# Planner changes in a threshold-attention and GELU kernel: weight loads in one chain, tied to later pairs, and other ranks

## The chip, the cores and the metric

The kernel runs on one core of a Trainium2 chip. The metric is the device time of one execution in microseconds (us). The kernel before takes 1434.29 us, the median of three runs (1433.63 to 1434.62). A profile of one execution gives a span of 1431.2 us.

A core has five engines that run side by side: TensorE (PE, matrix products), VectorE (DVE), ScalarE (ACT), GpSimd (POOL) and SyncE (SP). Here GpSimd issues the loads of the weights, and SyncE nearly all other transfers. Each engine runs its own list of instructions; semaphores make one wait for another.

## What is computed

```python
# attention: batch 8, heads 8, sequence 576, head_dim 64, float32
scores = q @ k.transpose(0, 1, 3, 2) / sqrt(64)
thresh = max(scores, axis=-1) - tau
scores = where(scores >= thresh, scores, -1e9)
scores = scores - max(scores, axis=-1)
attn = exp(scores);  attn = attn / (sum(attn, axis=-1) + 1e-9)
a = attn @ v
# bridge: heads side by side -> x of 4608 tokens x 512
h = x @ w_in                        # 512 x 2048
g = h * 1 / (1 + exp(-1.702 * h))
out = g @ w_out                     # 2048 x 512
```

Both weights arrive as 64-bit floats. The kernel itself turns them into 32-bit ones.

## The kernel before

Two heads make a pair, and there are 32 pairs, 4 to a batch element. For each pair the kernel transposes q and k (VectorE), makes the transposed scores (TensorE) in four tiles of 128 keys and a tail of 64 per head, copies them to SBUF (ScalarE), reduces the maxima (VectorE), sends the threshold row through DRAM to all partitions (SyncE; pairs 0 to 7), subtracts it (VectorE), masks with a steep Prelu and takes the exponential (ScalarE), multiplies with v and, for pairs 0 to 4, with ones for the denominators (TensorE), and places the scaled result in `xT` (VectorE). Whenever 512 tokens are complete, a block of the feed-forward part follows: 64 matmuls with w_in, 16 GELUs, 64 matmuls with w_out.

The Python program first lists all pieces of work as tasks and then runs a planner, a small event simulation with an assumed cost for each task. Whenever an engine of the simulation is free, the ready task with the lowest rank is emitted on it. The planner thus decides the order of instructions on each engine, once, while the program is built. The waits on the chip come from the data that instructions share, not from the planner's edges.

```python
    limits = {"psA": 3, "psM": 2, "s_m": 8, "s_t": 2, "io": 2, "xT": 3, "mb": 1,
              "raw0": 1, "raw1": 1, "qkT0": 1, "qkT1": 1, "v_m": 2, "w64": 2, "mbt": 1, "row": 1, "kd": 1}
    # ... cut ...
    EARLY = {
        "lower_rows": -1.16,
        "values": 0.42,
        "exps": 0.63,
        "load_qk": -0.91,
        "prep": -1.45,
        "load_v": 0.65,
        "over_groups": -1.04,
        "sub": -0.29,
    }
    LATER = {"in_groups": 0.38}

    def task(engine, cost, rank, f, *a, after=(), take=(), give=(), lag=0.06):
        if 0 <= rank < LAST:
            rank += (EARLY if a[0] < 2 * NPAIR else LATER).get(f.__name__, 0.0)
        tasks.append((engine, cost, rank, f, a, [x for x in after if x is not None],
                      take, give, lag))
        return len(tasks) - 1
```

A piece of weights (128 x 512 elements) is loaded twice, the second time shifted by three bytes, and converted in four steps: exponent bits (VectorE), power of two (ScalarE), fraction (two VectorE instructions), product (VectorE). Sixteen pieces belong to w_in and sixteen to w_out. The loads land in four staging areas, which lie in the still unused `w_out`, or in two buffers `w64`:

```python
    def load_w(i):
        # ... cut: t and t3 are a staging area or a w64 buffer ...
        nc.gpsimd.dma_start(out=t.rearrange("p c w -> p (c w)"), in_=dram.bitcast(U32))
        nc.gpsimd.dma_start(
            out=t3.rearrange("p c w -> p (c w)").bitcast(U8)[:, 0 : 8 * WC - 3],
            in_=dram.bitcast(U8)[:, 3 : 8 * WC],
        )
    # ... cut ...
    ready_w = []
    for i in range(len(pieces)):
        rank = 3.61 + 0.42 * i / n_in if i < n_in else 4.11 + 0.57 * (i / n_in - 1)
        # ... cut ...
        x = stage(i)
        place = ("w64",) if x is None else (f"stage{x}",)
        a = task("POOL", 2.4, rank, load_w, i, take=place, lag=5.0)
        e = task("DVE", 0.43, rank, cv_ex, i, after=[a])
        m = task("ACT", 0.79, rank, cv_power, i, after=[e])
        a = task("DVE", 1.14, rank, cv_frac, i, after=[e])
        over = [ready_w[y] for y in range(i) if i >= n_in and stage(y) == (i - n_in) // PER_STAGE]
        ready_w.append(task("DVE", 0.7, rank - 1.01, cv_end, i, after=[a, m] + over, give=place))
```

Loads and transposes of a pair, and its softmax:

```python
        lq = task("SP", 2.0, r - 2.0, load_qk, n, 0, q0, take=own(n, "raw0"), lag=2.0)
        lk = task("SP", 2.0 if n else 0.1, r - 2.0, load_qk, n, 1, q1, take=own(n, "raw1"), lag=2.0)
        lv = task("SP", 2.1, r - 1.2, load_v, n, take=("v_m",), lag=2.0)
        pq = task("DVE", 0.77, r, prep, n, 0, after=[lq], take=own(n, "qkT0"), give=own(n, "raw0"))
        pk = task("DVE", 0.77, r, prep, n, 1, after=[lk], take=own(n, "qkT1"), give=own(n, "raw1"))
        # ... cut: scores, copies, maxima, threshold row ...
            a = task("DVE", ..., r, sub, n, t, after=subs[-1:], ...)
            a = task("ACT", 0.68 if tail else 1.16, r, mask, n, t, after=[a])
            ws.append(task("ACT", 0.87 if tail else 1.34, r, exps, n, t, after=[a]))
```

The scratch of pairs 1 and 3 lies in the still unused `gT`, so the profile shows their tiles under that name. Matmuls are `L344` and `L337` (scores, `ps`), `L476` (values `pv` and denominators `den`), `L555` (w_in, `hps`) and `L574` (w_out, `ops`).

Of the kernel before, what the change touches and what calls it, by code (L numbers as in the profile page):

```python
# [30 lines left out]
def kernel(  # L31
# [32 lines left out]
    NPAIR = H // 2  # L64
    NKT = 4
# [18 lines left out]
    psA = ctx.enter_context(tc.tile_pool(name="psA", bufs=3, space=bass.MemoryType.PSUM))  # L84
# [6 lines left out]
    kd = const.tile([P, P], FP32, name="kd")  # L91
    v_t = [const.tile([P, 2, D], FP32, name=f"v_t{i}") for i in range(2)]
# [13 lines left out]

    tasks = []
    limits = {"psA": 3, "psM": 2, "s_m": 8, "s_t": 2, "io": 2, "xT": 3, "mb": 1,
              "raw0": 1, "raw1": 1, "qkT0": 1, "qkT1": 1, "v_m": 2, "w64": 2, "mbt": 1, "row": 1, "kd": 1}
    for x in ("raw0", "raw1", "qkT0", "qkT1", "mb"):  # L110
        limits[x + "_apart"] = 1
    limits["s_m_apart"] = NKT
# [1 line left out]


    EARLY = {
        "lower_rows": -1.16,
        "values": 0.42,
        "exps": 0.63,
        "load_qk": -0.91,  # L120
        "prep": -1.45,
        "load_v": 0.65,
        "over_groups": -1.04,
        "sub": -0.29,
    }
    LATER = {"in_groups": 0.38}

    def task(engine, cost, rank, f, *a, after=(), take=(), give=(), lag=0.06):
        if 0 <= rank < LAST:
            rank += (EARLY if a[0] < 2 * NPAIR else LATER).get(f.__name__, 0.0)  # L130
# [70 lines left out]
    def own(n, *pools):  # L201
        return tuple(x + "_apart" for x in pools) if n in APART else pools
# [33 lines left out]
    n_in = len(pieces)  # L236
# [294 lines left out]
    def cuts(b):  # L531

        return sorted({0, SH, S} | {x for x in range(-b * S % BLK, S, BLK)})
# [89 lines left out]
    BY_DMA = 8  # L623
    LEAD = 6

    ready_w = []
# [58 lines left out]
    for n in range(NP):  # L685
        gate = per_pair * (n - LEAD)
        after = ffn[gate : gate + 1] if gate >= 0 else []
        r = float(n)

        slow = 1.2 if n < NPAIR else 1.0  # L690
        q0, q1 = (nc.sync, nc.scalar) if n == 0 else (nc.sync, nc.sync)
        lq = task("SP", 2.0, r - 2.0, load_qk, n, 0, q0, take=own(n, "raw0"), lag=2.0)
        lk = task("SP", 2.0 if n else 0.1, r - 2.0, load_qk, n, 1, q1, take=own(n, "raw1"), lag=2.0)
        lv = task("SP", 2.1, r - 1.2, load_v, n, take=("v_m",), lag=2.0)
        pq = task("DVE", 0.77, r, prep, n, 0, after=[lq], take=own(n, "qkT0"), give=own(n, "raw0"))
        pk = task("DVE", 0.77, r, prep, n, 1, after=[lk], take=own(n, "qkT1"), give=own(n, "raw1"))
        pd = task("ACT", 0.5, r, prep_kd, n, after=[pk], take=("kd",))
        mx = []
        for t in range(NKT + 1):
            tail = t == NKT  # L700
            copies = []
            for c in range(1 if tail else 2):

                a = task(
                    "PE", (0.97 if tail else 0.53) * slow, r, scores, n, t, c,
                    after=[pq, pk] + ([pd] if tail else []) + after,
                    take=("psA", "s_t") if tail else ("psA",) + (own(n, "s_m") if c == 0 else ()),
                    give=own(n, "qkT0", "qkT1") + ("kd",) if tail else (),
                )
                after = [a]  # L710
                copies.append(task("ACT", 0.65, r, keep, n, t, c, after=[a], give=("psA",)))
            mx.append(task("DVE", 0.76 if tail else 1.37, r, in_groups, n, t, ALU.max, after=copies))
        a = task("DVE", 0.78, r, over_tiles, n, ALU.max, after=mx)
        a = task("DVE", 0.78, r, over_groups, n, ALU.max, after=[a])
        if n < BY_DMA:
            a = task("DVE", 0.5, r, lower_rows, n, after=[a, tau_done], take=("row",))
            a = task("SP", 0.35, r, row_out, n, after=[a], lag=2.3)
            m = task(
                "SP", 1.5, r, row_in, n, after=[a], take=own(n, "mb") + ("mbt",), give=("row",),
                lag=4.0,  # L720
            )
        else:
            a = task("DVE", 0.7, r, lower, n, after=[a, tau_done])
            m = task("DVE", 1.38, r, spread_max, n, after=[a], take=own(n, "mb"))
        ws, subs = [], [m]
        for t in range(NKT + 1):
            tail = t == NKT
            a = task(
                "DVE", (0.76 if n < BY_DMA else 1.5) if tail else 1.36, r, sub, n, t, after=subs[-1:],
                give=own(n, "mb") + (("mbt",) if n < BY_DMA else ()) if tail else (),  # L730
            )
            subs.append(a)
            a = task("ACT", 0.68 if tail else 1.16, r, mask, n, t, after=[a])
            ws.append(task("ACT", 0.87 if tail else 1.34, r, exps, n, t, after=[a]))
        back = own(n, "s_m") * NKT + ("s_t",)
        every = range(NKT + 1)
        if n < NPAIR:

            pv = den = None
            for t in every:  # L740
                first = t == 0
                den = task(
                    "PE", 1.1 * slow, r, sums_by_pe, n, [t], True, after=[ws[t], den],
                    take=("psM", "psM") if first else (),
                )
                pv = task(
                    "PE", 1.1 * slow, r, values, n, [t], after=[ws[t], den, pv, lv],
                    take=("psA",) if first else (), give=(back[t],) if t < NKT else ("s_t", "v_m"),
                )
            a = task("DVE", 1.22, r, one_row, n, after=[den], give=("psM", "psM"))  # L750
        else:
            pv = task("PE", 4.85, r, values, n, every, after=ws + [lv], take=("psA",), give=("v_m",))
# [53 lines left out]
```

## Time and profile before

| engine | busy us | share of the span |
|---|---|---|
| TensorE | 1380.6 | 96% |
| VectorE | 970.2 | 68% |
| ScalarE | 658.9 | 46% |
| GpSimd | 35.8 | 3% |

Each matmul with w_in or w_out shows as two records of 0.43 us each. The page cuts the span into 40 slices of 35.8 us. In them TensorE is busy 3, 7, 7 and 9 tenths, and from there on 9 (that is, 90% or more) in nearly every slice. So the first 120 us, in which the first pairs are worked on and the weights are loaded and converted, are the only stretch with much idle time on TensorE.

A line of the profile by groups names the source line, the engine, the operation, what it writes and reads, and how often. A line of waits names the waiting engine and instruction and, behind the arrow, what ended the wait.

### The profile page before, as it was taken

What the parts mean: (1) busy time and instruction counts of PE and PEld (TensorE: products, weight loads), DVE (VectorE), ACT (ScalarE), POOL (GpSimd) and SP (SyncE); (2) the same over time, 40 slices, a digit from 0 to 9 for tenths busy, and PEclk for the clock granted to TensorE, in tenths of its full rate; (3) what the DMA queues carried; (4) which work ended last, traced back from release to release, by engine and by line L of the source; (5) the groups of instructions that cost most, each with busy time, mean ns of one, the idle gap of its engine ahead of it and who ended that gap; (6) DMA issues with size and microseconds to landing.
All of it is one profiled execution on the core that took longest, in us unless ns stands there. A gap on an engine that the chain in (4) does not pass through costs nothing.

```text
span 1431.2 us, 13710 instructions
## 1 busy us (share of the span) xinstructions
PE 1380.6 (96%) x4936; PEld 650.2 (45%) x4936; DVE 970.2 (68%) x1629; ACT 658.9 (46%) x886; POOL 35.8 (3%) x78
## 2 busy tenths in 40 slices
PE   3779989999999999999999999999999999999998
PEld 2344434444444444444444444444444444444443
DVE  3999999888778888888887887788778710100200
ACT  3786655555455555555555554455445500100100
POOL 2012220000000000000000000000000000000000
PEclk8999999999999999999999999999999999999999
DMA  9468673211111111111111111111110000000000
GB/s 246 99 191 259 204 254 94 67 33 25 33 40 33 26 25 40 33 33 25 33 40 33 25 31 34 40 25 25 33 40 8 1 8 22 0 7 22 0 7 22
DMA packets 205707, 79.31 MB, mean 55 GB/s; under 512 B 192840, under 2 KB 192840, under 8 KB 205640
## 3 DMA queue, kind: packets, MB, share of 16 engines
q1 hardware_dynamic: 196072, 44.60, 14.4%
q0 software_dynamic: 7200, 33.55, 6.6%
q8 instruction: 39, 0.64, 0.2%
q10 hardware_dynamic: 2368, 0.30, 0.1%
q14 instruction: 28, 0.23, 0.1%
HBM read 68.93 MB, written 9.47 MB: 55 GB/s over the span
## 4 chain that ended last, share of the span: by engine, by line
PE 88%; DVE 6%; SPq 2%; DMA 2%; ACT 1%; issue 1%; DVEq 0%; ACTq 0%
PE ops L574 34%; PE hps L555 34%; PE pv L476 9%; PE ps L344 9%; PE ps L337 2%; SPq L214 2%; DVE s_m L447 1%; DVE part L377 1%; DMA mb<-row 1%; ACT gT L462 1%; ACT gT L458 1%; DMA row<-flat 0%; PE den L476 0%; DVE w_in L309 0%; DVE gT L447 0%
## 5 line engine op out<-in xcount | busy, mean ns | idle before, releaser
L574 PE MATMUL ops<-w_out,gT 128*128 128x512 f32 x1152 | 507.8, 596 | 5.0 <-DVE w_out L309 5.0
L555 PE MATMUL hps<-xT,w_in 128*128 128x512 f32 x1152 | 506.4, 595 | 0.3 <-DVE gT L566 0.3
L377 DVE TRANSPOSE_TENSOR_REDUCE part<-s_m 128x36 f32<-128x1152 f32 x228 | 303.5, 1358 | 101.8 <-ACT s_m L363 96.8
L574 PEld LDWEIGHTS ops<-w_out,gT 128*128 128x128 f32 x1152 | 216.2, 190 | 273.8 <-issue 263.5
L555 PEld LDWEIGHTS hps<-xT,w_in 128*128 128x128 f32 x1152 | 216.3, 190 | 267.9 <-issue 256.4
L566 DVE SCALAR_TENSOR_TENSOR gT<-th,hps 128x512 f32<-128x512 f32 x144 | 97.5, 677 | 234.8 <-ACT th L563 234.2
L363 ACT COPY s_m<-ps 128x576 f32<-128x576 f32 x240 | 138.8, 650 | 155.4 <-PE ps L344 153.9
L563 ACT ACTIVATE th<-hps 128x512 f32<-128x512 f32 x144 | 85.2, 592 | 217.4 <-PE hps L555 191.6
L458 ACT ACTIVATE s_m<-s_m 128x1152 f32<-128x1152 f32 x120 | 137.6, 1153 | 62.5 <-DVE s_m L447 62.1
L462 ACT ACTIVATE s_m<-s_m,shift,scl 128x1152 f32<-128x1152 f32 x120 | 160.5, 1343 | 2.4
L447 DVE TENSOR_TENSOR s_m<-s_m,mb 128x1152 f32<-128x1152 f32 x120 | 156.2, 1351 | 5.0 <-DMA mb<-row 4.3
L344 PE MATMUL ps<-qkT 64*128 64x288 f32 x960 | 144.6, 432 | 12.7 <-DVE qkT L320 12.2
L581 ACT ACTIVATE osb<-ops 128x512 f32<-128x512 f32 x36 | 21.4, 594 | 233.5 <-PE ops L574 233.3
L344 PEld LDWEIGHTS ps<-qkT 64*128 64x128 f32 x960 | 83.9, 189 | 91.4 <-issue 52.5
L476 PE MATMUL pv<-s_m,v_m 128*64 128x288 f32 x960 | 124.9, 413 | 0.0
L476 PEld LDWEIGHTS pv<-s_m,v_m 128*64 128x64 f32 x960 | 67.2, 138 | 64.0 <-issue 12.6
L377 DVE TRANSPOSE_TENSOR_REDUCE part_t<-s_t 128x18 f32<-128x576 f32 x59 | 44.2, 749 | 0.7 <-ACT s_t L363 0.2
L543 DVE TENSOR_TENSOR xT<-pv,rc 128x288 f32<-128x288 f32 (+8 forms) x96 | 28.3, 350 | 17.0 <-PE pv L476 15.7
L337 PE MATMUL ps<-qkT,kd 128*128 128x288 f32 x120 | 36.8, 429 | 0.3 <-ACT s_m L363 0.3
L476 PE MATMUL pv<-s_t,v_t 128*64 128x288 f32 x256 | 36.5, 406 | 0.0
L452 DVE TENSOR_TENSOR s_t<-s_t,mb 64x576 f32<-64x576 f32 x48 | 36.0, 749 | 0.3
L325 ACT COPY kd<-qkT 64x64 f32<-64x64 f32 x60 | 14.5, 241 | 45.6 <-DVE qkT L320 45.2
(81 smaller groups left out, 621.4 us busy)
## 6 DMA issues: line engine op xcount, KB each, us to landing
out_dram<-osb SPq DMA_DIRECT2D x36, 256.0 KB, 2.0
q_raw<-in_q_dram SPq DMA_DIRECT2D x120, 72.0 KB, 2.2
k_raw<-in_k_dram SPq DMA_DIRECT2D x116, 72.0 KB, 2.3
v_m<-in_v_dram SPq DMA_DIRECT2D x64, 128.0 KB, 2.4
w_out<-in_moe_w_in_dram POOLq DMA_DIRECT2D x12, 512.0 KB, 9.1
w<-in_moe_w_out_dram POOLq DMA_DIRECT2D x12, 512.0 KB, 4.8
w_out<-in_moe_w_in_dram POOLq DMA_DIRECT2D x12, 511.6 KB, 10.0
w64s<-in_moe_w_out_dram POOLq DMA_DIRECT2D x12, 511.6 KB, 5.8
```

The costliest lines, as they stand in the source:

```text
L337: nc.tensor.matmul(ps[:, i, 0:SH], lhsT=kd, rhs=qT[:, ts(i, SH)], start=True, stop=True,)
L344: nc.tensor.matmul(ps[:, h, 0:SH], lhsT=kT[ts(h, D), ts(t, P)], rhs=qT[ts(h, D), ts(c, SH)], start=True, stop=True,)
L363: nc.scalar.copy(out=o, in_=pss.pop((n, t, c))[:, :, 0:SH])
L377: nc.vector.tensor_reduce(out=o, in_=i, axis=AXL.X, op=op, apply_transpose=True)
L447: nc.vector.tensor_tensor(out=s, in0=s, in1=mb, op=ALU.subtract)
L458: nc.scalar.activation(out=s, in_=s, func=AF.Prelu, alpha=STEEP)
L462: nc.scalar.activation(out=s, in_=s, func=AF.Exp, scale=scl, bias=shift)
L476: nc.tensor.matmul(o[c][ts(h, D), 0:SH], lhsT=lhsT, rhs=rhs, start=(t == 0), stop=(t == NKT),)
L555: nc.tensor.matmul(hidden[j], lhsT=w_in[:, c, ts(j, P)], rhs=xTs[blk][:, c, :], start=(c == 0), stop=(c == NDC - 1),)
L563: nc.scalar.activation(out=ths[j], in_=hidden[j], func=AF.Tanh, scale=GELU_SCALE / 2)
L566: nc.vector.scalar_tensor_tensor(out=gT[j], in0=ths.pop(j), scalar=1.0, in1=hidden.pop(j), op0=ALU.add, op1=ALU.mult)
L574: nc.tensor.matmul(acc[i], lhsT=gT[j][:, ts(i, P)], rhs=w_out[:, j, :], start=(j == 0), stop=(j == NFC - 1),)
```

## The change

It touches the planner alone: ranks, assumed costs, and edges between tasks.

- Every weight load gets an edge from the load before it. In the planner the first three also wait for the transposed k of the third pair (n = 2), and the next three for that of the fourth (n = 3). This is meant to keep the weights out of the way of the first pairs.
- The ranks of all weight work are new, and the final product no longer runs ahead of its piece's rank.
- The table of rank offsets for the first eight pairs has new values and two new entries.
- The planner learns of buffers that it did not count: `rc` and the two `v_t`. The assumed cost of value and denominator matmuls of the first four pairs and the assumed latency of the threshold row are raised.

```diff
     limits = {"psA": 3, "psM": 2, "s_m": 8, "s_t": 2, "io": 2, "xT": 3, "mb": 1,
-              "raw0": 1, "raw1": 1, "qkT0": 1, "qkT1": 1, "v_m": 2, "w64": 2, "mbt": 1, "row": 1, "kd": 1}
+              "raw0": 1, "raw1": 1, "qkT0": 1, "qkT1": 1, "v_m": 2, "w64": 2, "mbt": 1, "row": 1, "kd": 1, "rc": 1, "v_t0": 1, "v_t1": 1}
     EARLY = {
-        "lower_rows": -1.16,
+        "lower_rows": -1.89,
         "values": 0.42,
         "exps": 0.63,
         "load_qk": -0.91,
         "prep": -1.45,
-        "load_v": 0.65,
-        "over_groups": -1.04,
+        "load_v": 1.46,
+        "mask": 0.88,
+        "over_groups": -1.9,
         "sub": -0.29,
+        "one_group": 0.95,
     }
 ... cut: an empty table CV is added ...
-        rank = 3.61 + 0.42 * i / n_in if i < n_in else 4.11 + 0.57 * (i / n_in - 1)
+        rank = 3.04 + 0.51 * i / n_in if i < n_in else 2.15 + 2.2 * (i / n_in - 1)
-        a = task("POOL", 2.4, rank, load_w, i, take=place, lag=5.0)
+        a = task("POOL", 2.4, rank, load_w, i, after=w_loads[-1:], take=place, lag=5.0)
+        w_loads.append(a)
-        ready_w.append(task("DVE", 0.7, rank - 1.01, cv_end, i, after=[a, m] + over, give=place))
+        ready_w.append(task("DVE", 0.7, rank, cv_end, i, after=[a, m] + over, give=place))
-        lv = task("SP", 2.1, r - 1.2, load_v, n, take=("v_m",), lag=2.0)
+        lv = task("SP", 2.1, r - 1.2, load_v, n, take=("v_m", v_tail), lag=2.0)
+        if n in (2, 3):
+            for a in w_loads[3 * (n - 2) : 3 * (n - 1)]:
+                tasks[a][5].append(pk)
-            a = task("SP", 0.35, r, row_out, n, after=[a], lag=2.3)
+            a = task("SP", 0.35, r, row_out, n, after=[a], lag=2.8)
             m = task(
                 "SP", 1.5, r, row_in, n, after=[a], take=own(n, "mb") + ("mbt",), give=("row",),
-                lag=4.0,
+                lag=5.0,
             )
-                    "PE", 1.1 * slow, r, sums_by_pe, n, [t], True, after=[ws[t], den],
+                    "PE", 1.32 * slow, r, sums_by_pe, n, [t], True, after=[ws[t], den],
-                    "PE", 1.1 * slow, r, values, n, [t], after=[ws[t], den, pv, lv],
+                    "PE", 1.32 * slow, r, values, n, [t], after=[ws[t], den, pv, lv],
-        a = task("DVE", 1.07, r, spread_sums, n, after=[a])
+        a = task("DVE", 1.07, r, spread_sums, n, after=[a], take=("rc",))
-            "DVE", 1.1, r, place_x, n, after=[a, pv], take=("xT",) * len(new), give=("psA",)
+            "DVE", 1.1, r, place_x, n, after=[a, pv], take=("xT",) * len(new), give=("psA", "rc")
 ... cut: the same buffers are given back with v_tail in two more places ...
```

More of the change, by code (lines that the diff above doesn't have):

```diff
@@ L121 @@
         "prep": -1.45,
-        "load_v": 0.65,
-        "over_groups": -1.04,
+        "load_v": 1.46,
+        "mask": 0.88,
+        "over_groups": -1.9,
         "sub": -0.29,
+        "one_group": 0.95,
     }
-    LATER = {"in_groups": 0.38}
+    LATER = {
+        "in_groups": 0.38,
+    }
+    CV = {
+    }
     def task(engine, cost, rank, f, *a, after=(), take=(), give=(), lag=0.06):
         if 0 <= rank < LAST:
-            rank += (EARLY if a[0] < 2 * NPAIR else LATER).get(f.__name__, 0.0)
+            rank += CV.get(f.__name__, 0.0) + (EARLY if a[0] < 2 * NPAIR else LATER).get(f.__name__, 0.0)
         tasks.append((engine, cost, rank, f, a, [x for x in after if x is not None],
@@ L624 @@
     LEAD = 6
-    ready_w = []
+    ready_w, w_loads = [], []
     for i in range(len(pieces)):
-        rank = 3.61 + 0.42 * i / n_in if i < n_in else 4.11 + 0.57 * (i / n_in - 1)
+        rank = 3.04 + 0.51 * i / n_in if i < n_in else 2.15 + 2.2 * (i / n_in - 1)
         if not wide:
@@ L693 @@
         lk = task("SP", 2.0 if n else 0.1, r - 2.0, load_qk, n, 1, q1, take=own(n, "raw1"), lag=2.0)
-        lv = task("SP", 2.1, r - 1.2, load_v, n, take=("v_m",), lag=2.0)
+        v_tail = f"v_t{n % 2}"
+        lv = task("SP", 2.1, r - 1.2, load_v, n, take=("v_m", v_tail), lag=2.0)
         pq = task("DVE", 0.77, r, prep, n, 0, after=[lq], take=own(n, "qkT0"), give=own(n, "raw0"))
         pk = task("DVE", 0.77, r, prep, n, 1, after=[lk], take=own(n, "qkT1"), give=own(n, "raw1"))
+        if n in (2, 3):
+            for a in w_loads[3 * (n - 2) : 3 * (n - 1)]:
+                tasks[a][5].append(pk)
         pd = task("ACT", 0.5, r, prep_kd, n, after=[pk], take=("kd",))
@@ L746 @@
                 pv = task(
-                    "PE", 1.1 * slow, r, values, n, [t], after=[ws[t], den, pv, lv],
-                    take=("psA",) if first else (), give=(back[t],) if t < NKT else ("s_t", "v_m"),
+                    "PE", 1.32 * slow, r, values, n, [t], after=[ws[t], den, pv, lv],
+                    take=("psA",) if first else (), give=(back[t],) if t < NKT else ("s_t", "v_m", v_tail),
                 )
@@ L751 @@
         else:
-            pv = task("PE", 4.85, r, values, n, every, after=ws + [lv], take=("psA",), give=("v_m",))
+            pv = task("PE", 4.85, r, values, n, every, after=ws + [lv], take=("psA",), give=("v_m", v_tail))
         if NPAIR <= n < BY_PE:
```

## The prediction

> **What bounds the kernel now.** I read the page first. TensorE is busy 1380.6 of 1431.2 us, so at most 50.6 us can be won by any reordering that leaves its work alone. Next I asked in which stretch those 50.6 us lie (busy time of each engine by stretch; first the stretch, its length, then busy us and instructions of TensorE, its weight loads, VectorE, ScalarE and GpSimd, granted clock, share of the DMA engines, GB/s):
>
> ```profile
> 0.00:30.00 30.00, 8.37 (x38) 5.68 (x39) 7.00 (x14) 8.38 (x15) 8.23 (x26) 0.89 0.94 268
> 30.00:60.00 30.00, 22.69 (x146) 13.65 (x148) 27.13 (x41) 21.32 (x32) 0.00 (x0) 0.89 0.53 121
> 60.00:90.00 30.00, 21.60 (x146) 11.63 (x144) 28.73 (x49) 25.37 (x33) 2.12 (x4) 0.97 0.54 140
> 90.00:117.80 27.80, 25.46 (x178) 13.28 (x175) 26.73 (x56) 23.46 (x28) 6.34 (x12) 0.91 0.49 152
> 117.80:150.00 32.20, 30.70 (x95) 14.43 (x94) 29.21 (x56) 14.78 (x26) 4.56 (x9) 1.00 0.84 278
> 185.00:215.40 30.40, 25.36 (x77) 11.53 (x76) 27.46 (x50) 19.36 (x26) 6.37 (x12) 0.93 0.68 240
> 260.00:1431.20 1171.20, 1167.27 (x3954) 542.90 (x3950) 748.75 (x1247) 502.52 (x674) 0.00 (x0) 1.00 0.12 26
> ```
>
> The reader is to see three things. Up to 117.8 us TensorE idles 21.6 + 7.3 + 8.4 + 2.3 = 39.7 us. From 117.8 to 260 us it idles only about 7.1 us (1.5, 0.3, 5.0, 0.2). After 260 us it idles 3.9 us, all behind its last matmul (the last store). And from 30 us on VectorE is over 90% busy, until 117.8 us and beyond: in the head it is VectorE that sets the pace. The waits of TensorE name the releasers, over the whole run (us in all, times, longest):
>
> ```profile
> PE ps L344 <- DVE qkT L320: 12.2, 3, 10.5
> PE den L476 <- ACT s_m L462: 11.5, 4, 5.7
> PE ps L344 <- DVE gT L320: 11.1, 1, 11.1
> PE ops L574 <- DVE w_out L309: 5.0, 1, 5.0
> ```
>
> The 11.1 us are pair 1's transposes, and behind those stands a transfer. VectorE in order of time (start, us, what, and in brackets the idle time before and its releaser):
>
> ```profile
> 26.58 0.78 DVE L320 STREAM_TRANSPOSE gT<-gT 128x576 f32<-128x576 f32 x1 [11.71 <-DMA gT<-in_q_dram]
> ```
>
> And GpSimd, whose instructions issue the weight loads:
>
> ```profile
> 2.46 0.53 POOL L272 DMA_DIRECT2D w_out<-in_moe_w_in_dram  x1
> ...
> 13.93 0.54 POOL L273 DMA_DIRECT2D w64s<-in_moe_w_in_dram  x1 [0.84 <-DMA w_out<-in_moe_w_in_dram]
> 70.96 0.53 POOL L272 DMA_DIRECT2D w_out<-in_moe_w_in_dram  x1 [56.50 <-DVE w_out L283]
> ```
>
> Pair 1's q lands only at 26.6 us, while six pieces of w_in (two transfers of 512 KB each) are issued between 2.5 and 14 us, at 94% busy DMA engines. The seventh waits for a staging buffer.
>
> **What the Trainium skill says.** "TensorE: Matmul & The Clock Gate" (Step-by-step: what each phase is for) says that TensorE is the only engine that reorders, and there only its weight loads. So an instruction put too early on VectorE or ScalarE blocks all behind it; the trace agrees: 11.71 us before pair 1's transpose, though max reductions of pair 0 stand ready behind it. "DMA: Bandwidth & Descriptors" (Issuing engines are not separate DMA queues) says that transfers of all issuing engines interleave on the same 16 DMA engines; the 94% beside pair 1's late q agrees. "TensorE: Matmul & The Clock Gate" (HAM oscillation — how this bites in real kernels) says that a TensorE gap over about 3.4 us costs slow clock afterwards. The trace agrees: after the 5.0 us gap at 208 us, two ops records take 2.08 us where others take 0.43 each, and the 32 pv records 5.23 us where they take 4.10 elsewhere: 2.3 us more.
>
> **The change, part by part.** The body of every instruction stays. Only the planner, which runs while the program is built, gets other ranks, costs and dependences; what reaches the chip is another order on each engine.
>
> *The tie to k of pairs 2 and 3.* It is an edge of the planner only: a GpSimd load has no data in common with pair 2's k, so no wait is emitted. In the two programs the first twelve weight transfers on GpSimd have the same order and waits (none, then the completion of earlier transfers of that queue), and the SyncE queue begins with the same transfers. So the six loads still go out at 2.5 to 14 us, and pair 1's q still lands at about 26.6 us. Of the 21.6 us idle before 30 us the tie wins nothing. It does make the planner believe in weights after pair 3's k, and so place their conversion later.
>
> *The head on VectorE, 26.6 to 117.8 us.* I walk the new order with the old durations (start to start: max reduction 1.26, subtraction 1.26, a pair's reciprocal row 2.07, exponent 0.33, fraction 1.08, final product 0.61, three placing products 0.80). Pair 1's tail reduction (0.67) moves into the 2.06 us wait for pair 0's mask row, so pair 1's threshold is ready 0.7 us sooner, and pair 3's transposes end at 67.9 instead of 68.5. Then come four exponents and three fractions, 4.6 us: 72.5, against three, two and one product (3.8 us; 72.3) before. Masks and exponentials now alternate on ScalarE (2.44 us per tile), so pair 1's softmax ends at about 72.5 instead of 71.9 and the tail reduction starts at 73.1 against 72.4. Three products and pair 1's placing end at 80.6; the score matmuls of pair 3 wait for pair 1's accumulator (80.0), as before (78.5). Pair 2's subtraction starts at 83.3, or up to 85 as its mask row now shares the DMA engines with three reloads released at 78 to 80 us; before 81.9. I take 84.2. Then 5.7 subtraction, 5.3 reductions and fold to 95.3; weights 3.5; pair 2's reciprocal row 98.7 to 100.8; 1.7 of weights; pair 3's subtractions with placing to 109.0; then 9.0 us of weights in one run, to 118.0; row 120.1, one fraction, pair 3 placed at 122.0. Before: 119.6. The difference is not slower work but more of it: ahead of pair 3's placing stand 11 exponents, 11 fractions and 10 products, against 9 of each: 2 x 0.33 + 2 x 1.08 + 0.61 = 3.4 us.
>
> *The first w_in matmul* stands behind the same matmuls in both programs (scores of five pairs, denominators and values of four). With pair 3's exponentials stretched by four weight powers it starts at about 122.6 instead of 117.8: **+4.8 us**.
>
> *From there to 260 us.* Before, weights were converted late: waits of 1.5 (pair 5's transposes), 0.3, 5.0 (a w_out piece at 213.4) and 0.2, with 2.3 of slow clock: 9.3 us. Now 18 w_in matmuls run at once (15.5 us) and cover pair 5's transposes (about 136 against a need at 138). The 16 w_out pieces move up: twelve stand in order before the last GELU product (about 185), the others before about 211, while the matmuls that need pieces 14 and 15 come at about 212. The 5 us wait goes. The price is VectorE between GELU products: 2.1 us for a piece, at times 1.3 more, of a budget of 3.44 us per four w_in matmuls. With two accumulators I allow 2.0 us of waits. **-9.3 + 2.0 = -7.3 us.**
>
> *After 260 us* TensorE already runs without a gap, so nothing there can gain, and the new planner limits on rc and v_t only restate buffers that the program has anyway: 0.
>
> Sum: 4.8 - 7.3 = -2.5; 1434.3 - 2.5 = **1432 us**.
>
> **Rivals.**
> 1. *The tie works on the chip*: pair 1's q lands at 15 us, VectorE saturates some 11 us sooner, and the run ends near 1421. For it: the 11.71 us wait. Against: no wait in the new program carries it.
> 2. *The w_out rush stalls TensorE.* Conversions now ride on every GELU product, and each reload waits for the previous product of its buffer (1.07 us to issue, 4.8 to 5.8 to land). If transfers lag by 1 us per piece, TensorE loses 10 to 15 us in the first w_in pass: about 1443. For it: the same product, exponent, reload loop already spaces loads 5.5 us apart before. Against: the planner's 7.4 us for a load is longer than the 6.4 or so measured.
> 3. *ScalarE's alternation brings denominators forward*: they waited 11.5 us on exponentials. If that counted, 5 us less: 1427. Against: the work of the pair's softmax is the same in sum, and VectorE, not TensorE, is what is late in the head.
>
> **Range and chances.** The gain cannot exceed 46.7 us of gaps ahead of the last matmul, of which 21.6 precede any use of what changed; faster by over 28.7 us would need nearly all the rest. Slower by 28.7 us would need every second GELU product late by over 3 us. So within 2% is nearly sure: faster 0.01, same 0.97, slower 0.02. My walk may be off by 3 us in the head and 5 in the w_out stretch: 1424 to 1441.
>
> **What would show it.** Right: pair 1's q still lands at 26 to 27 us; first w_in matmul at 121 to 125; no wait on a w_out product of over 1 us; at most 4 us of TensorE idle between the first w_in matmul and 260 us; nothing changed beyond. Wrong: pair 1's transposes before 20 us (rival 1), waits of TensorE on GELU products summing to over 6 us (rival 2), or a first w_in matmul before 117 (rival 3 or an error of my walk).

## The result, and the profile after

The changed kernel takes 1432.36 us, the median of four runs (1431.78 to 1433.64), against 1434.45 us (1433.63 to 1435.32) for the kernel before beside it: a ratio of 0.9987 with a 95% interval of 0.9969 to 1.0004. The prediction was 1432.0 us in a range of 1424 to 1441. Measured again on another chip ("The changed kernel once more", below) the ratio is 0.9967, interval 0.9955 to 0.998. So there is a gain: 0.1% in the first measurement, whose interval includes none, and 0.3% in the second, whose interval does not.

The table by stretch of the changed kernel, with the columns of the one of before (stretch, its length, busy us and instructions of TensorE, its weight loads, VectorE, ScalarE and GpSimd, granted clock, share of the DMA engines, GB/s):

```profile
0.00:30.00 30.00, 8.80 (x38) 6.09 (x40) 7.10 (x13) 8.05 (x15) 8.26 (x26) 0.92 0.94 269
30.00:60.00 30.00, 22.68 (x136) 14.06 (x136) 26.39 (x42) 21.68 (x29) 0.00 (x0) 0.80 0.55 120
60.00:90.00 30.00, 23.71 (x156) 12.66 (x152) 28.68 (x51) 24.29 (x30) 3.17 (x6) 0.94 0.51 140
90.00:117.80 27.80, 22.79 (x140) 11.08 (x142) 26.52 (x52) 24.11 (x28) 5.60 (x11) 0.82 0.73 229
117.80:150.00 32.20, 31.95 (x122) 15.53 (x119) 30.70 (x56) 17.94 (x31) 6.87 (x14) 1.00 0.73 235
185.00:215.40 30.40, 29.95 (x148) 14.61 (x147) 29.04 (x53) 14.60 (x21) 4.48 (x8) 1.00 0.66 197
260.00:1430.50 1170.50, 1166.08 (x3974) 542.83 (x3973) 752.98 (x1250) 505.87 (x678) 0.00 (x0) 1.00 0.12 25
```

The first three rows differ little from before; the fourth holds fewer TensorE records, 140 instead of 178. The row from 185 us on is another: TensorE is busy 29.95 of 30.40 us where it was busy 25.36, at full clock. The tail from 260 us is as it was, with 4.4 us idle against 3.9.

The waits of TensorE in the changed kernel (us in all, times, longest):

```profile
PE ps L350 <- DVE qkT L326: 12.2, 1, 12.2
PE den L482 <- ACT s_m L468: 10.3, 6, 6.3
PE ps L350 <- DVE gT L326: 9.0, 1, 9.0
PE den L482 <- ACT gT L468: 5.6, 4, 2.3
PE hps L561 <- DVE gT L572: 1.9, 1, 1.9
```

No wait on a product of w_out is left. In its place stands one wait of 1.9 us on a GELU product (`hps`). The late q and the early weight loads of the head are still there. VectorE, and GpSimd with the weight loads, in order of time:

```profile
26.37 0.78 DVE L326 STREAM_TRANSPOSE gT<-gT 128x576 f32<-128x576 f32 x1 [9.80 <-DMA gT<-in_q_dram]
```

```profile
2.46 0.53 POOL L278 DMA_DIRECT2D w_out<-in_moe_w_in_dram  x1
...
13.90 0.54 POOL L279 DMA_DIRECT2D w64s<-in_moe_w_in_dram  x1 [0.85 <-DMA w_out<-in_moe_w_in_dram]
80.24 0.54 POOL L278 DMA_DIRECT2D w_out<-in_moe_w_in_dram  x1 [65.81 <-DVE w_in L315]
```

Pair 1's q is transposed at 26.37 us (before 26.58), and six pieces go out between 2.46 and 13.90 us, as before. The tie to pairs 2 and 3 left no trace on the chip.

The ledger, from stretches cut at the first w_in matmul (117.82 us before, 123.62 us after; same columns as above). The kernel before:

```profile
0.00:117.82 117.82, 78.14 (x500) 44.24 (x501) 89.61 (x157) 78.52 (x105) 16.70 (x42) 0.91 0.63 170
117.82:260.00 142.18, 135.14 (x487) 63.09 (x487) 131.87 (x227) 77.85 (x108) 19.14 (x36) 0.98 0.65 205
```

The changed kernel:

```profile
0.00:123.62 123.62, 83.55 (x501) 47.04 (x502) 94.27 (x168) 81.91 (x107) 18.87 (x46) 0.88 0.69 196
123.62:260.00 136.38, 134.08 (x464) 62.37 (x463) 122.96 (x212) 75.09 (x103) 17.89 (x32) 1.00 0.59 185
```

The head grew by 5.8 us. TensorE runs the same 500 or so records in it, but VectorE has 4.7 us more work ahead of that point (94.27 against 89.61) and ScalarE 3.4 us more. That alone does not name the cause: a longer stretch holds more work, and VectorE is busy 76% of it in both. What the end of the head waits for is read below, at the walk of the head. From there to 260 us TensorE idles 2.3 us (136.38 - 134.08) instead of 7.0, and what it runs is at full clock. Behind the first w_in matmul the span is 1430.5 - 123.62 = 1306.9 us against 1431.2 - 117.82 = 1313.4 us, so 6.5 us are won there. In these two profiles 5.8 - 6.5 leaves -0.7 us; the medians say -2.1.

### The profile page after: what moved, and what is told of

It reads as the page before. It is cut to its first block, busy times and chain, and to the rows that moved or that the text cites. A ratio compares the mean times of both kernels' runs of the same rounds, so it can differ in the third digit from the quotient of the medians.

```text
span 1430.5 us, 13702 instructions
## 1 busy us (share of the span) xinstructions
PE 1383.7 (97%) x4936; PEld 652.2 (46%) x4936; DVE 970.2 (68%) x1629; ACT 662.9 (46%) x886; POOL 36.8 (3%) x78
## 3 DMA queue, kind: packets, MB, share of 16 engines
q1 hardware_dynamic: 196072, 44.60, 14.5%
## 4 chain that ended last, share of the span: by engine, by line
PE 88%; DVE 6%; SPq 2%; DMA 2%; ACT 2%; issue 1%; DVEq 0%; ACTq 0%
PE ops L580 34%; PE hps L561 34%; PE pv L482 9%; PE ps L350 8%; PE ps L343 2%; SPq L220 2%; DVE part L383 1%; DVE s_m L453 1%; DMA mb<-row 1%; ACT gT L468 0%; DVE gT L453 0%; PE den L482 0%; DMA row<-flat 0%; ACT gT L464 0%; DVE part_t L383 0%
## 5 line engine op out<-in xcount | busy, mean ns | idle before, releaser
L427 DVE STREAM_TRANSPOSE mb<-thr 128x1152 f32<-128x1152 f32 x24 | 33.1, 1378 | 0.8
```

## The experiments

The theory to test: the tie does nothing on the chip; the head grew because more weight work stands in it, on VectorE, which sets its pace; and the ranks of the weights took the wait on w_out away. All ratios are to the kernel before on the same chip, whose median was 1435.9 to 1436.5 us there. "Distance" is the time from pair 1's first score matmul to the first w_in matmul: it leaves out the start, which shifts by up to 2.0 us between the kernels without a gate. It is 117.82 - 29.83 = 88.0 us before and 123.62 - 29.54 = 94.1 us after.

**The changed kernel with the old ranks of the weights** (the diff goes from the changed kernel to this one):

```diff
-        rank = 3.04 + 0.51 * i / n_in if i < n_in else 2.15 + 2.2 * (i / n_in - 1)
+        rank = 3.61 + 0.42 * i / n_in if i < n_in else 4.11 + 0.57 * (i / n_in - 1)
-        ready_w.append(task("DVE", 0.7, rank, cv_end, i, after=[a, m] + over, give=place))
+        ready_w.append(task("DVE", 0.7, rank - 1.01, cv_end, i, after=[a, m] + over, give=place))
```

> The changed kernel with the weight ranks of before (w_in 3.61 + 0.42 i/n, w_out 4.11 + ..., final product 1.01 earlier); chain, tie and all else stay. Theory (the gain after the first w_in matmul comes from the earlier w_out conversions alone): ahead of the last GELU product stand 26 final products as before, not 28, and ahead of pair 3's placing 11, not 10; so the first w_in matmul at about 124 us as in the changed kernel, and the wait of the ops matmuls on a w_out product returns with about 5 us, and 2 us of slow clock behind it: 1437 to 1440 us. Rival (the offsets of masks and reductions made the gain, the weight ranks nothing): 1431 to 1433 us and no such wait.

Measured: 1436.38 us, ratio 1.0, interval 0.9992 to 1.0008: the gain is gone. The head stayed long (first w_in matmul at 124.92 us, distance 94.5). But the wait did not come back at a w_out product. TensorE in order of time (start, us, what, and the idle time before it):

```profile
223.01 1.24 PE L350 MATMUL ps<-qkT 64*128 64x288 f32 x8 [3.48 <-DVE qkT L326]
224.79 6.47 PE L350 MATMUL ps<-qkT 64*128 64x288 f32 x24 [0.54 <-ACT s_m L369]
```

It is now pair 6's transposes that come late on VectorE: a wait of 3.48 us, then 0.54 us for a copy of ScalarE, and behind them 24 records take 6.47 us where 24 take 3.34 elsewhere, at a granted clock of 0.50 to 0.53 from 225 to 231.3 us (the first eight records behind the gap are not slow yet). This agrees with what the Trainium skill says in "TensorE: Matmul & The Clock Gate" (HAM oscillation — how this bites in real kernels) of gaps over about 3.4 us. So the new ranks carry the gain, but not by freeing one named wait: with the late weights VectorE is full there (94% busy from 215 to 231.3 us), and which piece of its work arrives late there depends on the other ranks.

**The kernel before with the edges alone** (chain and tie):

```diff
+        a = task("POOL", 2.4, rank, load_w, i, after=w_loads[-1:], take=place, lag=5.0)
+        w_loads.append(a)
...
+        if n in (2, 3):
+            for a in w_loads[3 * (n - 2) : 3 * (n - 1)]:
+                tasks[a][5].append(pk)
```

> The kernel before with only the edges among and into the weight loads added to the planner. Theory (the edges are the planner's alone and only reorder): pair 1's q still lands at 26 to 27 us; ahead of pair 3's placing stand 10 exponents, 9 fractions, 9 products (9, 9, 9 before), so the first w_in matmul comes within 2 us of 117.8; the 5 us wait on a w_out product stays; 1433 to 1437 us. Rival (the tie keeps weight transfers out of the first pairs' way): pair 1's q before 20 us, 1421 to 1427 us.

Measured: 1433.9 us, ratio 0.9985, interval 0.9978 to 0.9992. The first w_in matmul comes at 120.58 us, 2.8 us later than before and a little outside what was expected; pair 1's transposes still wait 11.6 us. The wait on w_out stays, as the waits of TensorE show:

```profile
PE ops L574 <- DVE w_out L309: 6.8, 3, 4.2
```

So the edges alone do not cure the w_out wait, and are still worth some 2 us. The later first w_in matmul is no loss in itself: 524 records of TensorE stand ahead of it instead of 500, and TensorE idles 37.2 us up to it instead of 39.7. Behind it the span is 1429.7 - 120.58 = 1309.1 us, 4.3 us less than before.

**The changed kernel without its edges** (the tie and the chain taken out of the planner):

```diff
-        a = task("POOL", 2.4, rank, load_w, i, after=w_loads[-1:], take=place, lag=5.0)
+        a = task("POOL", 2.4, rank, load_w, i, take=place, lag=5.0)
-        if n in (2, 3):
+        if False:
```

> The changed kernel without the edges among and into the weight loads; ranks, offsets, limits and costs as changed. Theory (the edges work through the plan: without them the new ranks pull weights forward, 20 products instead of 13 stand ahead of the first GELU product): TensorE waits 8 to 15 us for GELU products after its first w_in matmuls, 1439 to 1448 us. Rival (the edges do nothing that counts): 1431 to 1434 us.

Measured: 1452.95 us, ratio 1.0114, interval 1.0101 to 1.0128. It is slower by more than expected, and the place is another. The waits of TensorE:

```profile
PE ps L350 <- DVE qkT L326: 21.9, 2, 11.0
PE hps L561 <- DVE w_in L315: 5.9, 1, 5.9
PE hps L561 <- DVE gT L572: 1.6, 3, 0.9
```

Not the GELU products are late (1.6 us), but pair 5's transposes, 10.95 us at 137 us, and a w_in product at 151.8 us. Without the tie the planner expects weights early, and with the new low ranks of w_out it lets 20 products run ahead of the first GELU product, where the changed kernel has 13. So an edge that puts no wait on the chip still is worth 1.0114 against 0.9967: by the order it makes the planner choose.

**The changed kernel once more**, for a second measurement of it:

> The changed kernel itself beside the others, for a narrower interval. Theory (the edges alone gave what there is): ratio to before 0.998 to 0.999, the same as the edges alone (0.9985). Rival (the ranks and offsets add their own): 0.997 or less.

Measured: 1431.81 us, ratio 0.9967, interval 0.9955 to 0.998. Its first stretch against the one shown above:

```profile
0.00:123.94 123.94, 80.70 (x501) 45.24 (x502) 94.25 (x168) 81.40 (x107) 18.88 (x46) 0.88 0.68 195
```

TensorE was busy 80.70 us here and 83.55 us in the other profile with the same records, yet the first w_in matmul comes at 123.94 and 123.62 us. The mean granted clock is 0.88 in both, so it does not show the difference; single stretches do. From 106.7 to 112.6 us the clock was 0.71 in the first profile and TensorE busy 5.81 us with 32 records, here 1.00 and 3.98 us with 30. In these two profiles the slower clock there takes time in which TensorE would otherwise wait for exponentials, and does not move the head's end. VectorE's work is the same to 0.02 us.

**A real gate, on both ties.** What the tie seems meant for can be put on the chip: GpSimd copies one element of pair 2's transposed k into the staging area ahead of load 0, and one of pair 3's ahead of load 3. The load overwrites the element, so it has to wait for the copy, and the copy for the transpose.

```diff
+        if i in GATE:
+            nc.gpsimd.tensor_copy(out=t[0:1, 0, 0:1].bitcast(FP32), in_=k_of[GATE[i]][0:1, 0:1])
         nc.gpsimd.dma_start(out=t.rearrange("p c w -> p (c w)"), in_=dram.bitcast(U32))
```

with `GATE = {0: 2, 3: 3}`.

> The changed kernel with the tie made real: GpSimd copies one element of pair 2's transposed k into the first staging buffer ahead of its load, and one of pair 3's ahead of the fourth load, so the chip has to wait as the planner assumed. Theory (the 11 us late q of pair 1 comes from the weight transfers, and VectorE's work sets the head): pair 1's q lands by 14 us, TensorE's wait for pair 1 falls from 9 us to under 2, everything of the head comes 9 to 11 us earlier less a wait of up to 4 us for the fourth piece; 1422 to 1427 us. Rival (the per-pair chain of mask row, exponentials and denominators sets the head, not VectorE's load): under 4 us gained, 1428 to 1432 us.

Measured: 1427.34 us, ratio 0.9947, interval 0.9934 to 0.9961. Pair 1's transposes move from 26.4 to 12.8 us, but the first w_in matmul only to 118.49 us: VectorE then waits 10.43 us for pair 1's mask row. SyncE issues that row only at 41.10 us, behind pair 4's q and k (11.10 and 5.46 us to issue), and its broadcast at 52.09 us; the second three pieces of weights go out from 39.11 us on.

**The gate on pair 2's k alone**, `GATE = {0: 2}`:

> As the last, with only the first wait: all six loads go out one after the other once pair 2's k is transposed. Theory: no wait for the fourth piece, first w_in matmul at 113 to 115 us, 1421 to 1424 us. Rival 1 (chain of latencies): 1428 to 1432 us. Rival 2 (the six loads now collide with the mask rows of pairs 0 and 1, which then land 3 us later each): 1425 to 1428 us, with waits on the mask rows of over 5 us.

Measured: 1425.35 us, ratio 0.9925, interval 0.9913 to 0.9936; first w_in matmul at 116.58 us. Pair 1 starts 13 us sooner, but the head ends only 7 us sooner than in the changed kernel. SyncE, which issues the transfers, in order of time (start, us to issue them, what):

```profile
5.79 2.15 SPq L220 DMA_DIRECT2D gT<-in_q_dram  x4
...
24.68 14.14 SPq L220 DMA_DIRECT2D q_raw<-in_q_dram  x4
38.87 9.78 SPq L220 DMA_DIRECT2D k_raw<-in_k_dram  x4
48.75 0.36 SPq L442 DMA_DIRECT2D row<-flat  x1
```

and VectorE:

```profile
54.21 2.63 DVE L460 TENSOR_TENSOR gT<-gT 128x1152 f32<-128x1152 f32 x2 [8.64 <-DMA gT<-row]
```

Now the weights go out at 22.9 to 36.3 us, and it is pair 4's q and k that SyncE issues beside them: four q transfers, which take 2.15 us to issue alone, take 14.14 us, and those of k 9.78. Pair 1's threshold row is ready at 37 us and stands behind them in SyncE's order until 48.75 us. The gate has moved the collision from pair 1's q to pair 1's row, much as the second rival had it.

**The gate, with the row ahead of pair 4's q, first attempt.** Only one edge was added, from pair 1's row to pair 4's q:

```diff
-        lq = task("SP", 2.0, r - 2.0, load_qk, n, 0, q0, take=own(n, "raw0"), lag=2.0)
+        lq = task("SP", 2.0, r - 2.0, load_qk, n, 0, q0, after=[rin[n - 3]] if n in (4,) else [], take=own(n, "raw0"), lag=2.0)
```

> The changed kernel with all six first weight loads really waiting for pair 2's transposed k, and with an edge that puts pair 4's q and k loads behind pair 1's mask row on SyncE. Theory (with the gate alone, the row of pair 1 was held up because SyncE sat in pair 4's loads, whose packets queue beside the weights): VectorE's wait for that row falls from 8.6 us to under 3, first w_in matmul at 108 to 111 us, 1416 to 1420 us where before takes 1434. Rival (the row lands late because the weights saturate the DMA engines, whatever stands ahead of it): wait still over 6 us, 1423 to 1426 us.

Measured: 1438.62 us, ratio 1.0024, interval 1.0014 to 1.0033, and the question stays unanswered: the planner put pair 5's q and k into the gap (13.62 and 9.66 us to issue), so that the row still stood behind them, and pair 4 came late. Its row wait is 7.38 us, and a w_out product is waited for 6.1 us at 200 us.

**The same with q and k kept in order of pairs:**

```diff
+        lq = task("SP", 2.0, r - 2.0, load_qk, n, 0, q0, after=([rin[1]] if n == 4 else []) + ([lk] if n > 4 else []), ...)
+        lk = task("SP", 2.0 if n else 0.1, r - 2.0, load_qk, n, 1, q1, after=[lq] if n > 3 else [], ...)
```

> As the gate on pair 2's k alone, and on SyncE pair 1's mask row ahead of pair 4's q and k, now with q and k loads kept in order so that pair 5's cannot slip in between (they did in the run before of this kind, which so did not test the point). Theory: VectorE's wait for that row falls from 8.6 us to under 2, first w_in matmul at 107 to 110 us, ratio to before 0.986 to 0.989 (about 1416 to 1419 us where before takes 1435). Rival (the row is late because weights fill the DMA engines): wait over 5 us and a ratio of 0.991 or more.

Measured: **1419.12 us, ratio 0.9876, interval 0.9855 to 0.9896**, better than both kernels; first w_in matmul at 110.65 us, a little later than expected. SyncE:

```profile
37.19 0.28 SPq L442 DMA_DIRECT2D row<-flat  x1
42.59 0.36 SPq L451 DMA_DIRECT2D gT<-row  x1
...
44.20 3.91 SPq L220 DMA_DIRECT2D q_raw<-in_q_dram  x4
48.15 2.39 SPq L220 DMA_DIRECT2D k_raw<-in_k_dram  x4
```

and VectorE:

```profile
48.28 2.63 DVE L460 TENSOR_TENSOR gT<-gT 128x1152 f32<-128x1152 f32 x2 [2.57 <-DMA gT<-row]
```

The row goes out at 37.19 us, the wait for it falls from 8.64 to 2.57 us (under 2 was expected), and pair 4's loads, now behind most of the weights, take 3.91 and 2.39 us to issue. What is left of the row's delay is its own way through DRAM beside the weights: 5.4 us from its issue to that of its broadcast. So the order in SyncE's list is most of the delay, and the rival a small part.

**The order of rows and loads without the gate** (the diff goes from the last kernel):

```diff
-    GATE = {0: 2}
-        if i in GATE:
-            nc.gpsimd.tensor_copy(out=t[0:1, 0, 0:1].bitcast(FP32), in_=k_of[GATE[i]][0:1, 0:1])
```

> The changed kernel with only the order of pair 1's mask row and pair 4's q and k swapped, without the real wait of the weights. Theory (the swap matters only where pair 4's loads run beside the weights): those loads take 4 us here and end long before the row is asked for, so within 1 us of the changed kernel, ratio 0.996 to 0.9985. Rival (the row's place alone is worth something): 0.994 or less.

Measured: 1431.64 us, ratio 0.9968, interval 0.9956 to 0.998, the same as the changed kernel (0.9967); distance 94.25 us. The order is worth nothing by itself, and something like 0.5% behind the gate.

**Less work on VectorE.** The second of the two fraction instructions is left out, 0.61 us for each of the eleven fractions ahead of pair 3's placing, 6.7 us in all. This kernel leaves out the weights' sign; the planner's order is unchanged.

```diff
-        nc.vector.scalar_tensor_tensor(
-            out=frac.bitcast(I32), in0=hi.bitcast(I32), scalar=31, in1=frac.bitcast(I32),
-            op0=ALU.arith_shift_right, op1=ALU.bitwise_xor,
-        )
```

> The changed kernel without the second fraction instruction of each weight piece, so the weights lack their sign; the planner's order stays. It takes 0.6 to 0.65 us of VectorE work off each piece, 7 us for the eleven ahead of pair 3's placing. Theory (VectorE's load sets the head): first w_in matmul 6 to 7 us earlier, 1425 to 1427 us. Rival (the chain of a pair through mask row, masks and exponentials on ScalarE and denominators limits the head just as much): 2 to 3 us earlier, 1429 to 1431 us, with new waits of VectorE on ScalarE or the row.

Measured: 1430.59 us, ratio 0.9962, interval 0.995 to 0.9975, no different from the changed kernel. The distance falls from 94.1 to 91.2 us, by 2.9 of the 6.7 us, as the rival had it. The waits of VectorE between 30 and 118 us:

```profile
DVE w_in L311 <- ACT w_out L297: 3.0, 4, 1.3
DVE part_t L379 <- ACT s_t L365: 3.0, 1, 3.0
```

In the changed kernel the same view has 0.5 and 0.8 us there. VectorE, made shorter, waits for ScalarE. Nor do all eleven fractions lie in the way of the first w_in matmul: six of them, 3.7 us, stand ahead of pair 3's subtractions; the other five run while ScalarE works on pair 3, which takes 14.4 us from the first subtraction to the end of the last exponential (14.5 in the changed kernel).

**Less work on ScalarE.** The Prelu of the mask is left out for pairs 0 to 3: 4 x 1.15 + 0.67 = 5.3 us per pair. This kernel leaves out the cut-off of small scores there.

```diff
-        nc.scalar.activation(out=s, in_=s, func=AF.Prelu, alpha=STEEP)
+        if n >= NPAIR:
+            nc.scalar.activation(out=s, in_=s, func=AF.Prelu, alpha=STEEP)
```

> The changed kernel without the mask (the steep Prelu) of pairs 0 to 3, so their scores below the threshold are not cut off; order as planned. It takes 1.1 us of ScalarE work off each of 16 tiles and 0.6 off each of 4 tails, 5 us a pair in the chain from the mask row to the denominators. Theory (after the run with less VectorE work: the head is a chain that alternates between VectorE and ScalarE, and ScalarE's softmax is part of it): first w_in matmul 4 to 8 us earlier than the 123.8 of the changed kernel, ratio 0.990 to 0.994. Rival (VectorE's load alone sets the head): under 2 us earlier, 0.9955 to 0.998.

Measured: 1430.01 us, ratio 0.9957, interval 0.9941 to 0.9973; distance 90.9 us, 3.2 less for some 21 us taken off ScalarE. The stretch from 60 to 90 us:

```profile
60.00:90.00 30.00, 23.25 (x148) 12.72 (x150) 29.54 (x51) 19.79 (x25) 3.16 (x6) 0.89 0.56 165
```

VectorE is busy 29.54 of 30 us (28.68 in the changed kernel), ScalarE 19.79 (24.29): now VectorE alone is full. Between 30 and 118 us ScalarE waits 4.8 + 3.5 us for VectorE's exponent bits, and pair 3, relieved of 5.3 us of masks, takes only about 1.2 us less from its first subtraction to its last exponential (13.3 us).

**Both cuts at once**, which leaves out the weights' sign and the cut-off for pairs 0 to 3:

```diff
-        nc.vector.scalar_tensor_tensor(out=frac.bitcast(I32), ..., op0=ALU.arith_shift_right, op1=ALU.bitwise_xor)
-        nc.scalar.activation(out=s, in_=s, func=AF.Prelu, alpha=STEEP)
+        if n >= NPAIR:
+            nc.scalar.activation(out=s, in_=s, func=AF.Prelu, alpha=STEEP)
```

> Both cuts at once: VectorE without the second fraction instruction, which leaves out the sign of the weights, and ScalarE without the Prelu for pairs 0 to 3, which leaves out the cut-off there. The distance from pair 1's first score matmul to the first w_in matmul is 94.1 us in the changed kernel, 91.2 with the first cut alone and 90.9 with the second alone. Theory: the head is a chain that passes back and forth between VectorE and ScalarE, and each cut alone is taken up in part by the other engine; then both together give clearly more than the sum of the parts (3 + 3 us): a distance of 87 us or less, and a ratio of 0.990 to 0.993. Rival: the two gains are independent pieces of one chain and simply add: about 88 us, ratio 0.993. Rival two: something else limits as well (rows through DRAM, the order itself), so that the second cut wins little on top of the first: a distance of 89.5 to 91 us, ratio 0.995 to 0.996.

Measured: 1423.47 us, ratio 0.9913, interval 0.9899 to 0.9927; first w_in matmul at 116.41 us with pair 1's scores at 30.54 us, a distance of 85.9 us. Together the cuts take 8.2 us off the distance, alone 2.9 and 3.2; against the changed kernel's 0.9967 the ratio falls by 0.0054, alone by 0.0005 and 0.0010. The distance of one and the same order came out at 94.1, 94.2 and 94.25 us in three profiles, so 8.2 against 6.1 is outside that scatter. But a part of each gain is not the cut's. VectorE had pair 0's mask row 4.16, 4.19 and 3.87 us after the issue of its broadcast in the profiles of the three cuts, and 5.34, 5.16 and 5.16 us in the three of the uncut order, although nothing that was cut runs before it; why it varies is open. From the subtraction behind that row to the first w_in matmul the uncut order takes 78.8 to 79.2 us, and the cuts win 2.1, 2.4 and, together, 6.9 us: still clearly more than the sum. The two engines pass the head back and forth, and what is cut from one alone is in good part taken up by waits for the other.

## Why the prediction was right

**Where the idle time lies** held: 40.1 us up to the first w_in matmul (39.7 before), 2.3 us from there to 260 us, 4.4 us after (3.9 before).

**The tie is the planner's alone** held: pair 1's q at 26.37 us against "about 26.6", the six loads unmoved. The real gates show what the first rival would have brought had the edge become a wait: 0.5 and 0.75%, and 1.2% with the row in front. The 1421 us given for that rival, 0.9%, was a fair size, but it overlooked that the weights then run into pair 4's loads and pair 1's row.

**The walk of the head** gave +4.8 us and measured +5.8. What the first w_in matmul stands behind is pair 3's softmax, by way of its denominators and values and pair 4's last scores in TensorE's order; it reads only pairs 0 and 1, and does not wait for pair 3's placing (before, that starts at 118.82 us, behind it). Pair 3's first subtractions, its last exponential and the first w_in matmul, each from its engine's list in order of time, in the kernel before:

```profile
99.12 3.85 DVE L447 TENSOR_TENSOR gT<-gT 128x1152 f32<-128x1152 f32 x3
110.38 0.85 ACT L462 ACTIVATE s_t<-s_t,shift,scl 128x576 f32<-128x576 f32 x1
117.82 1.88 PE L555 MATMUL hps<-xT,w_in 128*128 128x512 f32 x4
```

In the changed kernel, with the weight powers that stand between:

```profile
102.75 3.89 DVE L453 TENSOR_TENSOR gT<-gT 128x1152 f32<-128x1152 f32 x3
111.47 0.77 ACT L297 ACTIVATE w_out<-w_out,rebias 128x512 int32<-128x512 int32 x1
113.19 0.78 ACT L297 ACTIVATE w_out<-w_out,rebias 128x512 int32<-128x512 int32 x1
115.67 0.81 ACT L297 ACTIVATE w_out<-w_out,rebias 128x512 int32<-128x512 int32 x1
116.39 0.85 ACT L468 ACTIVATE s_t<-s_t,shift,scl 128x576 f32<-128x576 f32 x1
123.62 15.61 PE L561 MATMUL hps<-xT,w_in 128*128 128x512 f32 x36
```

The subtractions start 3.6 us later. Here the source that the prediction gave, "not slower work but more of it", holds, though it was counted at pair 3's placing: ahead of the subtractions stand 6 exponents, 6 fractions and 5 products against 4 of each, 3.4 us by the prediction's durations. From there to the end of the last exponential it is 14.5 us against 12.1, and the three weight powers, 2.4 us together, are the difference. From there to the first w_in matmul it is 6.4 us against 6.6. So 3.6 + 2.4 - 0.2 makes the 5.8 us. The second term was mis-sized: the walk has the subtractions at 102.5 us, 3.4 us later than before, and so leaves 1.4 us of its 4.8 for ScalarE's weight powers, where 2.4 were measured.

Point by point the walk is off elsewhere too. The transposes that the prediction called "pair 3's" at 67.9 us (and 68.5 before) are pair 4's; pair 3's are the two at 52 us. Those of pair 4 end at 69.05 us. The wait for pair 0's mask row, of which moving pair 1's tail reduction was to leave about 1.4 us, is 2.96 us even with the reduction ahead of it: VectorE has the row at 44.78 us, 5.3 us after its broadcast was issued (39.44 us), where before it took 3.8 us. The walk is 1.2 to 1.4 us late from there (the tail reduction at 74.45 us against 73.1); by pair 2's subtraction that is taken up (84.41 against 84.2). The last run of weights ahead of pair 3's placing takes 10.1 us where 9.0 were reckoned, 0.54 of it waiting for ScalarE, so that pair 3 is placed by 123.3 us (122.0).

**"In the head it is VectorE that sets the pace"** is the step that failed as it was put. Busy over 90% is not the same as setting the pace alone: taking 6.7 us off VectorE brought 2.9 us, taking 21 us off ScalarE 3.2, taking off both 8.2 (2.1, 2.4 and 6.9 us without the earlier mask row). It did little harm to the number, as the walk carried ScalarE's alternation of masks and exponentials along; had the change relieved VectorE alone, the same reasoning would have promised more than twice what comes.

**From the first w_in matmul to 260 us** -7.3 us was predicted and -6.5 us measured. The 5 us wait on w_out is gone, no w_out product is waited for, and the allowance of 2.0 us for waits is 2.3 us in the profile (1.9 of it one GELU product). The slow clock behind the old gap is gone too (1.00 from 185 us on). That the second rival's rush did little harm has to do with the edges: without them the same ranks cost 1.1%, by late transposes and a late w_in product and not by GELU products.

**The sum** is closer than the walk deserves. Its two terms are off by 1.0 and 0.8 us, both towards a slower kernel, so that these two profiles differ by -0.7 us and not by the predicted -2.5. The medians say -2.1 in one measurement and -4.3 in the other; that the first lies within 0.4 us of the forecast is luck.

**The third rival**, denominators sooner, did not happen: TensorE waits 10.3 + 5.6 us for exponentials, before 11.5 + 3.8. Pair 2's four tiles come 2.44 us apart in the changed kernel, one mask and one exponential each.

**The clock** was left out of the head's sum. There TensorE is busy 5.4 us longer than before for the same records (83.55 against 78.14). That is no term of the sum: the second profile of the same program has 80.70 us, and its head ends no sooner.

What stays open is which of the new ranks and costs lengthen the head. With the edges alone the subtractions of pair 3 start 71.3 us after pair 1's first score matmul, against 69.3 before and 73.2 in the changed kernel, and no weight power stands among pair 3's exponentials. With the old ranks of the weights the three powers do stand there, and the distance is 94.5 us. So the rest of the head's growth should lie with the table of offsets, the assumed costs and the new buffer limits, which were not tried one by one. The two terms of the walk are read from two traces; no run moves the three weight powers alone.

## What to carry to other kernels

An edge in a planner is a belief, not a wait: if a transfer is to stay out of the way on the chip, give it something to wait for, and then look which small transfer (here a mask row) stands behind large ones in the same issuing engine's order; here the change with both is 1.2% faster than the kernel before, without them 0.1 to 0.3%. Two engines that are 88 to 96% and 72 to 87% busy, as VectorE and ScalarE are here from 30 to 117.8 us, may limit a stretch together: shorten each alone and then both before naming the one that sets the pace. And count work up to the instruction that the end of the stretch waits for: work that runs beside the last link, as the five fractions beside pair 3's exponentials did here, can be cut without gain. Ranks and edges of such a planner are to be tried together: the rest of the change without the edges lost 1.1%, and the edges alone won 0.15%.

## What the runs showed of the hardware

- Issuing a transfer can hold its engine for long. The chain that ended last, in the changed kernel from 5 to 45 us (start, us, what), shows single issuing instructions of SyncE for pair 1's q that take 7.56 and 6.59 us beside the weight loads, where others of the same form take 0.50:

```profile
7.36 7.56 SPq L220
...
14.97 6.59 SPq L220
...
21.61 0.50 SPq L220
```

  The Trainium skill, in "DMA: Bandwidth & Descriptors" (Issuing engines are not separate DMA queues), calls the sequencer's time to start a DMA "usually small relative to the DMA itself". Here it was not: in the changed kernel the eight transfers of q for pairs 1 and 3 land 3.5 us after their issue in the median, and single issues took up to 7.56 us. With the gate on pair 2's k, four q transfers of pair 4 took 14.14 us to issue beside the weights and those of pair 1 2.15 us ahead of them. The measurements decide for this case; everything behind such issues on SyncE waited too.
- A threshold row's way out to DRAM took 5.4 us beside the weights (from its issue at 37.19 us to that of the broadcast at 42.59 us in the best version), and 1.8 us without them (21.00 to 22.80 us for pair 0 in the same run). With the gate on both ties it took 11.0 us (41.10 to 52.09 us).
- The granted clock in a stretch with many short waits differed between two executions of one program (0.71 and 1.00 from 106.7 to 112.6 us; over the whole head 83.55 and 80.70 us of TensorE time for the same records), and the end of the stretch moved by only 0.3 us.
